# A recurrent attention layer and a two-layer MLP on one core: one step's value products set beside the next step's scores, and PSUM banks dealt out anew

## The chip, the cores and the metric

The program runs on one core of a Trainium2 chip. A core has TensorE (PE: matmuls, with its weight loads PEld), VectorE (DVE), ScalarE (ACT), GpSimdE (POOL) and SyncE (SP, which issues most DMAs). Matmuls write to PSUM, which has eight banks; the other engines work in SBUF and, except POOL, read PSUM. Engines run side by side, each executes its own instructions in order, and semaphores let one wait for another. The metric is the device time of the whole program in microseconds (us); lower is better.

## The reference

For each of 4 x 8 (batch, head) pairs a matrix memory is carried over 768 positions, 40 numbers wide, and read by the query. The output goes through two matrix products with a softplus between them.

```python
for t in range(S):                                  # q, k, v, o_gate: (4, 8, 768, 40)
    m_new  = np.maximum(f_gate[:, :, t] + m, i_gate[:, :, t])
    f_stab = np.exp(f_gate[:, :, t] + m - m_new);  i_stab = np.exp(i_gate[:, :, t] - m_new)
    C = f_stab * C + i_stab * einsum('bhd,bhe->bhde', vt, kt)
    n = f_stab * n + i_stab * kt
    denom = np.maximum(np.abs(n . qt), 1.0)
    y[:, :, t] = sigmoid(o_gate[:, :, t]) * (C . qt) / denom
x = y.transpose(0, 2, 1, 3).reshape(3072, 320)      # tokens x (head, dim)
out = softplus(x @ w_in) @ w_out                    # 320 -> 2048 -> 320, float32
```

## The kernel before, in words

**Tiles and steps.** The 3072 tokens are cut into 24 steps of 128 tokens (one batch entry b, one chunk c, all 8 heads; a step is written b_c). Three steps make a tile of the MLP: 8 tiles, 0 to 7. The order of the steps is 1_0, 2_0, 0_0 (tile 0), 3_0, 0_1, 0_2 (tile 1), 0_3 and so on; from step number 4 on, the chunks of one batch entry follow each other, so each step needs the state that the one before it leaves.

**The MLP.** A tile passes through 16 units f. A unit of the first layer is 8 matmuls of 384 columns into one PSUM tile `hp` (L978). ACT takes the softplus twice (`gh`, L854, and in place, L855), DVE takes the rounding rest `gl` = hp - gh (L858). The second layer multiplies gh and gl into three PSUM tiles `po` (L949, 9 matmuls of 320 columns); it runs two units behind, so PE alternates hp of unit f and po of unit f - 2. In tile 0 there is no gl: one softplus, and po in plain float32 in pairs of units. In this text hp4_3 is unit 3 of tile 4, gl4_3 its rest. An hp bank is free again when gl has been written (in tile 0, when gh has).

**The attention of a step** after tile 0. DVE scans the decays (`pw`, L439) and weighs the gates (`gw`, L491), POOL scales the values (`v`, L482; `vw`, L500), DVE scales the queries (`mv`, L381). PE then multiplies the **score group** (`sp`, two banks: state products L600, scores L606, 32 matmuls). DVE weighs the scores into mv (L611, four instructions), and two carries of the state follow, each a product on POOL (L564) and a sum on DVE (L567); the second sum waits for POOL, and POOL for the first sum. Then PE multiplies the **value group** (`yq`, one bank, L642, 16 matmuls), ACT copies it (L659), it goes through DRAM and comes back transposed (L664 to L679), and DVE and ACT make the tile's X of it (L683 to L698).

**PSUM.** Three pools: ps_h with the tag hp, ps_o with po0 to po2, ps_a for the attention. Each gives its buffers out in turn; an allocation waits for the readers of the tile that had the buffer before. At the start ps_h also holds wm, six `fb` tiles and three transposes `xp` (L706, one for each step of tile 0), in this order, before hp0_0. In the record, float32 matmuls show as two entries each.

**What sets the order.** The program is written out once, each engine's order then being fixed (`in_order`, L113). `products` (L922) counts PE's slots n; every other piece of work is a generator with due times, and `tick(n)` lets those run that are due. A step has a base (Q["B.."] up to step 11, later Q["S0".."S2"] + NB of its tile) and a table of offsets (W from tile 3 on; M, N before) with an entry for each part: SP for the score group, YQ for the value group, YD, RD, NM, FIN for what becomes of it, FB for the fetch of the decays. `later_step` (L806) turns the offsets into events. The first tile follows a table of its own, F.

Of the kernel before, what the change touches and what calls it, by code (L numbers as in the profile page):

```python
# [16 lines left out]
PSUM = bass.MemoryType.PSUM  # L17

B, H, S, D = 4, 8, 768, 40
# [5 lines left out]
NS = sum(SIZES)  # L25
START = [sum(SIZES[:t]) for t in range(NT + 1)]
# [9 lines left out]
EP = 48  # L36
MID = 0
WIDE = 3
FIRST = [(1, 0), (2, 0), (0, 0), (3, 0)]
ORDER = FIRST + [(b, c) for b in range(B) for c in range(NC) if (b, c) not in FIRST]  # L40
UW = 640
# [3 lines left out]
def mlstm_moe_kernel(  # L45
# [20 lines left out]
    stage = ctx.enter_context(tc.tile_pool(name="stage", bufs=2))  # L66

    dpool = ctx.enter_context(tc.tile_pool(name="dpool", bufs=1, space=bass.MemoryType.DRAM))
    ps_h = ctx.enter_context(tc.tile_pool(name="ps_h", bufs=3, space=PSUM))
    ps_o = ctx.enter_context(tc.tile_pool(name="ps_o", bufs=1, space=PSUM))  # L70
    ps_a = ctx.enter_context(tc.tile_pool(name="ps_a", bufs=2, space=PSUM))

    nc.scalar.preload_act_table_set("natural_log_exp_and_others")

# [37 lines left out]
    @contextmanager  # L112
    def in_order():  # L113

        traced = nc.cur_bb.bb.instructions
        first = traced[-1]
        yield
        start = next(k for k in reversed(range(len(traced))) if traced[k] is first) + 1
        last = {}
        for ins in traced[start:]:  # L120
            if ins.engine in last:
                tc.add_manual_dep(
                    ins,
                    last[ins.engine].name,
                    mybir.DependencyInfo(mybir.DependencyClass.NoSync, mybir.DependencyReason.DATA),
                    reason="in_order",
                )
            last[ins.engine] = ins
# [156 lines left out]
    def lows():  # L285

        yield Q["LB"]
        for u in range(NF // 2):
            wol[u] = wl.tile([128, 2, DM], F32R, tag="wo", name=f"wol{u}")
            nc.vector.tensor_tensor(wol[u], wof[u], woh[:, 2 * u : 2 * u + 2, :], op=ALU.subtract)  # L290
            yield -1000 - Q["LS"]

    W = dict(FB=-80, LOAD=-67, Y=-29, SCAN=4, VI=11, VW=16, IQ=20, SP=24, SPD=12, CN=31, CD=36, CE=37, CF=42, YQ=53,
             YQD=-32, EV=15, YD=61, YD1=3, RD=96, RY=11, RZ=1, NM=138, FIN=146, XH=19, XL=18)
    M = dict(FB=-23, LOAD=-50, Y=-9, SCAN=3, VI=-10, VW=10, IQ=25, SP=27, SPD=12, CN=33, CD=43, CE=49, CF=50, YQ=54,
             YQD=3, EV=47, YD=69, YD1=-30, RD=79, RY=-95, RZ=26, NM=116, FIN=128, XH=-9, XL=15)
    N = dict(FB=-26, LOAD=-57, Y=-7, SCAN=9, VI=-16, VW=22, IQ=23, SP=28, SPD=8, CN=30, CD=34, CE=39, CF=60, YQ=55,
             YQD=6, EV=17, YD=67, YD1=-32, RD=84, RY=-22, RZ=10, NM=125, FIN=150, XH=-9, XL=14)
    Q = dict(Gi0=68, Go0=50, Gi1=-42, Go1=1, Gi2=-47, Go2=36, Gi3=38, Go3=7, Gi4=6, Go4=18, Gi5=-8, Go5=31, Gi6=-10,
             Go6=7, Gi7=4, Go7=35, B3=40, B4=84, B5=125, B6=260, B7=300, B8=368, B9=446, B10=528, S0=-375, S1=-292,  # L300
             S2=-195, GT=-381, GL=52, LB=214, LS=33, SPD=-12, OF0=1, OF1=19, GR0=25, GR1=82, GR2=29, GR3=-26, GR4=18,
             GR5=38, LG=10, FS0=-51, FS1=25, FSW=-14, CI=-48, CO=-4, CS=34, K0=-23, K1=-29, CF=15, RC=-17, RS=92,
             B2=-20, B11=620, GT2=92, GL2=108, FS2=-31, GR6=-1, Hi0=-20, Ji0=63, Hi1=34, Ji1=78, Hi2=16, Ji2=34,
             Hi3=-12, Ji3=49, Hi4=-8, Ji4=-16, Hi5=36, Ji5=136, Hi6=-16, Ji6=107, Hi7=-67, Ji7=20)
    CI = dict(A=-6, B=2, C=-54, D=-2, E=10, F=30)
    CO = dict(A=3, B=-52, C=15, D=12, E=-36)
# [17 lines left out]
    class Step:  # L324
        def __init__(self, s):
# [4 lines left out]
            self.n = f"{self.b}_{self.c}"  # L330
            self.at = (M, M, N, W)[min(self.t, WIDE)]
            self.late = self.t > 1
# [51 lines left out]
    def wide_gates(ts):  # L384

        yield 0
        for t in ts:
            load_gates(t)
        yield Q["GL"]
        nc.scalar.preload_act_table_set("sigmoid_and_others")  # L390
        for t in ts:
            nc.scalar.activation(eg[t], eg[t], AF.Sigmoid)
            done.add(("eg", t))
        nc.scalar.preload_act_table_set("softplus")
# [3 lines left out]
    def load_gates(t):  # L398
        g, n = SIZES[t], 128 * 3 * L
        eg[t] = p1.tile([128, NG, 3, L], F32, tag="eg", bufs=2, name=f"eg{t}")[:, 0:g]  # L400
        src = oT[START[t] * n : START[t + 1] * n]
        nc.sync.dma_start(eg[t], src.rearrange("(p g c l) -> p g c l", g=g, c=3, l=L))
# [312 lines left out]
    def first_tile(follow):  # L715
# [17 lines left out]
        def next_gates():  # L733
            for t in range(1, WIDE):
                load_gates(t)
                yield
            for t in range(1, WIDE):
                nc.scalar.activation(eg[t], eg[t], AF.Sigmoid)
                done.add(("eg", t))
            yield  # L740
# [65 lines left out]
    def later_step(z):  # L806
        yw, at = values_wide(z), z.at
        c0, c1 = carry(z, 0), carry(z, 1)

        def fetch():  # L810
            decays(z)
            load_values(z)
            unpark(z)

        def y():
            for r in yw:
                if r == "write":
                    return
                yield r

        ev = [
            (at["FB"], fetch),
            (at["LOAD"], lambda: load(z)),
            (at["Y"], lambda: load_inter(z)),
            (at["SCAN"], lambda: decay(z)),
            (at["VI"], lambda: gate_values(z)),
            (at["VW"], lambda: last_decays(z)),
            (at["VW"], lambda: state_values(z)),
            (at["SP"], lambda: scores(z)),
            (at["YQ"], y),  # L830
            (at["YD"], lambda: yw),
            (at["RD"], lambda: read_wide(z)),
            (at["NM"], lambda: finish_wide(z)),
            (at["FIN"], lambda: end_wide(z)),
        ]
        ev += [
            (at["IQ"], lambda: scale_queries(z)),
            (at["CN"], lambda: next(c0)),
            (at["CD"], lambda: next(c0, None)),
        ]  # L840
        if z.c < NC - 1:
            ev += [(at["CE"], lambda: next(c1)), (at["CF"], lambda: next(c1, None))]
        yield from in_turn(ev)
# [17 lines left out]
    def convert(u, i):  # L861
        g = (weights_out if i else weights)(u)
        for k, w in (CO if i else CI).items():
            yield w
            next(g, None)
            if k == "C":
                yield -1000 - Q["CF"]
                fetch_next()
# [5 lines left out]
    def first_states():  # L874
        for w, k in zip((Q["FS0"], Q["FS1"], Q["FS2"]), (1, 0, 2)):
            yield w
            z = zs[k]
            state(z)
            yield -1000 - Q["FSW"]
            for _ in new_state(z):  # L880
                pass

    NB = [NF * (8 * t + 3 * START[t]) for t in range(NT)]
# [3 lines left out]
    def start(g, base):  # L887
        nonlocal order
        order += 1
        resume(g, base, 0, order)  # L890

    def resume(g, base, at, k):
        try:
            r = next(g)
        except StopIteration:
            return
        at = at - r - 1000 if r <= -1000 else max(at, base + r)
        heapq.heappush(queue, (at, k, base, g))
# [111 lines left out]
    def finished(t):  # L1010
        return all(s in ended for s in range(START[t], START[t + 1]))

    def whole(z):
        yield from later_step(z)
        ended.add(z.s)

    with in_order():
        for k, (u, i) in enumerate(tensors[AHEAD:]):
            start(convert(u, i), Q[f"K{k}"] if k < 2 else Q["CO" if i else "CI"] + Q["CS"] * u)
        start(first_states(), 0)  # L1020
        start(lows(), 0)
        rest = [Step(s) for s in range(START[1], NS)]
        for s in range(START[1], NS):
            z = rest[s - START[1]]
            base = Q[f"B{s}"] if s < START[4] else Q[f"S{z.g}"] + NB[z.t]
            start(whole(z), base)
        for t in range(WIDE, NT):
            start(wide_gates([t]), NB[t] + Q["GT"])
        zs = first_tile(rest[:3])
        products()  # L1030
# [52 lines left out]
```

## Time and profile before

| | us |
|---|---|
| median of three runs | 461.8 (461.75 to 463.18) |
| profiled execution | 461.91 |
| its span in the profile | 460.2 |
| PE busy | 433.4 (94%) |
| PEld busy | 402.9 (88%) |
| DVE busy | 303.9 (66%) |
| ACT busy | 211.2 (46%) |
| POOL busy | 137.2 (30%) |

The span is cut into 40 slices of 11.5 us in the page's second part; PE's digits there are 5756799 and then 9 to the end. So PE has gaps in the first 80 us, where weights are converted and tile 0 is prepared, and hardly any after. The chain of work that ended last is 81% PE by the page's fourth part, 36% hp (L978) and 34% po (L949), and 9% DVE. Outside the span lie 1.7 us of the profiled execution. The granted clock of TensorE is given as a share: 1.00 is 2.4 GHz, 0.50 is 1.2 GHz.

### The profile page before, as it was taken

The numbers are of one execution on the slowest core, as the hardware profiler recorded it, in microseconds if no ns is written. First come the engines' busy times: TensorE is split into PE (matmuls) and PEld (weight loads), VectorE is DVE, ScalarE is ACT, GpSimd is POOL, SyncE is SP. The second block draws the span as 40 slices with busy tenths as digits, with TensorE's granted clock in tenths as the row PEclk, the third lists the DMA queues.
The fourth block names the chain that finished last, engine by engine and source line by source line (L and its number), as shares of the span: only waits on it lengthen the run. The fifth ranks groups of instructions, "written<-read, shape, count | busy, mean of one in ns | idle before, by whom it ended". The sixth has DMA issues, their size and how long they took to land.

```text
span 460.2 us, 10555 instructions
## 1 busy us (share of the span) xinstructions
PE 433.4 (94%) x4266; PEld 402.9 (88%) x4266; DVE 303.9 (66%) x577; ACT 211.2 (46%) x416; POOL 137.2 (30%) x152
## 2 busy tenths in 40 slices
PE   5756799899999999999999999999999999999997
PEld 4555587677999999999999999999999999999996
DVE  4657488998987967766776867656876678242121
ACT  2727778784233642355333733463333543333332
POOL 8646078455531131233122312302223111000000
PEclk9975999999999999999999999999999999999999
DMA  7954967587656564654464263555374220101001
GB/s 200 333 188 115 274 197 246 147 214 168 178 180 182 154 151 122 164 144 96 150 185 117 74 204 108 129 143 138 105 196 129 78 78 19 41 0 46 0 1 43
DMA packets 38139, 62.55 MB, mean 136 GB/s; under 512 B 5626, under 2 KB 20258, under 8 KB 38090
## 3 DMA queue, kind: packets, MB, share of 16 engines
q1 hardware_dynamic: 25958, 53.62, 41.3%
q10 hardware_dynamic: 12132, 8.26, 6.3%
q8 instruction: 33, 0.54, 0.5%
q14 instruction: 16, 0.13, 0.1%
HBM read 53.60 MB, written 8.26 MB: 134 GB/s over the span
## 4 chain that ended last, share of the span: by engine, by line
PE 81%; DVE 9%; ACT 3%; POOL 3%; issue 2%; DMA 0%; SPq 0%; POOLq 0%; DVEq 0%; ACTq 0%
PE hp L978 36%; PE po L949 34%; PE yq L642 4%; PE sp L606 2%; PE sp L600 2%; POOL v L564 1%; DVE wof L236 1%; PE yp L619 1%; PE wm L723 1%; DVE wih L271 1%; PE fb L455 1%; DVE wil L269 1%; DVE mv L611 1%; DVE nm L685 1%; DVE gw L494 1%
## 5 line engine op out<-in xcount | busy, mean ns | idle before, releaser
L978 PE MATMUL hp<-X,wih 128*128 128x384 f32 x768 | 181.7, 344 | 4.0 <-ACT X L708 2.8
L978 PEld LDWEIGHTS hp<-X,wih 128*128 128x128 f32 x768 | 133.9, 189 | 9.0 <-ACT X L708 3.2
L854 ACT ACTIVATE gh<-hp 128x384 fp32r<-128x384 f32 x112 | 55.0, 491 | 181.8 <-PE hp L978 175.0
L858 DVE TENSOR_TENSOR gl<-hp,gh 128x384 fp32r<-128x384 f32 x112 | 61.6, 555 | 74.0 <-ACT hp L855 73.1
L949 PE MATMUL po<-wol,gh 128*128 128x320 f32 x336 | 71.2, 311 | 0.0
L949 PE MATMUL po<-woh,gl 128*128 128x320 f32 x336 | 70.3, 309 | 0.0
L949 PE MATMUL po<-woh,gh 128*128 128x320 f32 x336 | 69.8, 308 | 0.0
L978 PE MATMUL hp<-X,wil 128*128 128x384 f32 x256 | 66.6, 339 | 0.1
L500 POOL TENSOR_TENSOR vw<-vt,gw 128x328 f32<-128x328 f32 x23 | 21.7, 944 | 134.3 <-DVE gw L491 123.0
L564 POOL TENSOR_TENSOR v<-v,flast 40x328 f32<-40x328 f32 x37 | 38.2, 1032 | 69.4 <-DVE v L567 53.7
L949 PEld LDWEIGHTS po<-woh,gh 128*128 128x128 f32 x336 | 57.3, 188 | 0.1
L949 PEld LDWEIGHTS po<-woh,gl 128*128 128x128 f32 x336 | 54.9, 188 | 0.2
L949 PEld LDWEIGHTS po<-wol,gh 128*128 128x128 f32 x336 | 54.5, 188 | 0.5
L855 ACT ACTIVATE hp<-hp 128x384 f32<-128x384 f32 x112 | 54.5, 487 | 0.0
L978 PEld LDWEIGHTS hp<-X,wil 128*128 128x128 f32 x256 | 46.4, 189 | 0.9 <-DVE wil L269 0.5
L611 DVE TENSOR_TENSOR mv<-sp,pw 64x256 f32<-64x256 f32 x84 | 31.8, 417 | 14.7 <-PE sp L606 14.2
L482 POOL TENSOR_TENSOR v<-vt,gT 64x328 f32<-64x328 f32 x42 | 33.6, 801 | 22.5 <-DMA vt<-in_vko 19.6
L381 DVE TENSOR_TENSOR mv<-mv,fc 64x512 f32<-64x512 f32 (+1 forms) x42 | 39.1, 930 | 1.1 <-DMA fc<-fc_d 0.5
L949 PE MATMUL po<-wof,gh 128*128 128x320 f32 x96 | 28.5, 440 | 3.9 <-ACT v L544 2.7
L567 DVE TENSOR_TENSOR v<-v,sp 40x164 f32<-40x164 f32 x74 | 23.9, 323 | 12.0 <-POOL v L564 10.7
L439 DVE TENSOR_TENSOR_SCAN pw<-fb,near 128x512 f32<-128x512 f32 x21 | 26.4, 1255 | 3.8 <-DMA fb<-fz_d 3.8
L949 PEld LDWEIGHTS po<-wof,gh 128*128 128x128 f32 x96 | 17.6, 189 | 10.8 <-ACT v L544 3.0
(126 smaller groups left out, 439.9 us busy)
## 6 DMA issues: line engine op xcount, KB each, us to landing
qk<-in_qk SPq DMA_DIRECT2D x21, 416.0 KB
vt<-in_vko SPq DMA_DIRECT2D x23, 324.0 KB
fb<-fz_d SPq DMA_DIRECT2D x42, 128.0 KB
wi<-in_wts SPq DMA_DIRECT2D x8, 640.0 KB
wo<-in_wts SPq DMA_DIRECT2D x8, 640.0 KB
eg<-in_oT SPq DMA_DIRECT2D x7, 576.0 KB
out<-ob SPq DMA_DIRECT2D x24, 160.0 KB
yd<-y ACTq DMA_DIRECT2D x36, 96.0 KB
```

What stands on the lines that cost most here:

```text
L381: nc.vector.tensor_tensor(z.mv[ch][r], z.mv[ch][r], z.fc[r], op=ALU.mult)
L439: nc.vector.tensor_tensor_scan(pw.rearrange(flat), fb.rearrange(flat), eye.rearrange(flat), 0.0, ALU.mult, ALU.add)
L482: nc.gpsimd.tensor_tensor(vi, v1[r], g[r], op=ALU.mult)
L500: nc.gpsimd.tensor_tensor(z.vw, v1, z.gw.broadcast_to([128, H, E]), op=ALU.mult)
L564: nc.gpsimd.tensor_tensor(heads(whole), old, f, op=ALU.mult)
L567: nc.vector.tensor_tensor(dst[i], dst[i], z.cps[ch][dims(i)], op=ALU.add)
L611: nc.vector.tensor_tensor(half(z.mv[ch][r], i), sps[i][r], half(z.pw[r], i), op=ALU.mult)
L854: nc.scalar.activation(gh, hp, AF.Softplus)
L855: nc.scalar.activation(hp, hp, AF.Softplus)
L858: nc.vector.tensor_tensor(gl, hp, gh, op=ALU.subtract)
L949: nc.tensor.matmul(po[j], a[:, j * 128 : (j + 1) * 128], w, start=first, stop=(last and left[j] == 0))
L978: nc.tensor.matmul(hp, a, r, start=(i == 0), stop=(i == len(seq) - 1))
```

## The change

Three things. First, ps_h gets two banks instead of three, ps_a three instead of two. Second, from step JOIN = 9 (the first of tile 3, 1_1) to step 22, the offsets YQ, YD, RD, NM and FIN of a step are moved by one common shift, so that its YQ falls on the SP of the next step: the two groups are then issued back to back. Third, bases and FB are set anew: B9, B10, B11 by -28, -32, -46 slots, S0, S1, S2 by -60, -52, -59, FB of the table W from -80 to -60.

```diff
+JOIN = 9
...
-    ps_h = ctx.enter_context(tc.tile_pool(name="ps_h", bufs=3, space=PSUM))
+    ps_h = ctx.enter_context(tc.tile_pool(name="ps_h", bufs=2, space=PSUM))
     ps_o = ctx.enter_context(tc.tile_pool(name="ps_o", bufs=1, space=PSUM))
-    ps_a = ctx.enter_context(tc.tile_pool(name="ps_a", bufs=2, space=PSUM))
+    ps_a = ctx.enter_context(tc.tile_pool(name="ps_a", bufs=3, space=PSUM))
...
-    W = dict(FB=-80, LOAD=-67, Y=-29, SCAN=4, VI=11, VW=16, IQ=20, SP=24, SPD=12, CN=31, CD=36, CE=37, CF=42, YQ=53,
+    W = dict(FB=-60, LOAD=-67, Y=-29, SCAN=4, VI=11, VW=16, IQ=20, SP=24, SPD=12, CN=31, CD=36, CE=37, CF=42, YQ=53,
...
+    def place(s):
+        z = rest[s - START[1]]
+        return Q[f"B{s}"] if s < START[4] else Q[f"S{z.g}"] + NB[z.t]
...
+    rest = [Step(s) for s in range(START[1], NS)]
...
         for s in range(START[1], NS):
             z = rest[s - START[1]]
-            base = Q[f"B{s}"] if s < START[4] else Q[f"S{z.g}"] + NB[z.t]
-            start(whole(z), base)
+            if s >= JOIN and s + 1 < NS:
+                shift = place(s + 1) + rest[s + 1 - START[1]].at["SP"] - place(s) - z.at["YQ"]
+                z.at = {**z.at, **{k: z.at[k] + shift for k in ("YQ", "YD", "RD", "NM", "FIN")}}
+            start(whole(z), place(s))
```

Line numbers after the change are one higher than before (L978 becomes L979). POOL's order is the same in both programs, and PE's order is the same up to hp1_10.

**Place 1, PE at the start of tile 0.** Before, with the semaphore that each row waits for; x0_0 is the third step's x, hp0_2 and hp0_3 are units of the first layer:

```order
L706 MATMUL xp2_0_355<-ident4_79,x2_0_352 128x128
L706 MATMUL xp2_0_355<-ident4_79,x2_0_352 128x128 [waits DVE_49]
L706 MATMUL xp0_0_369<-ident4_79,x0_0_349 128x128 [waits Activation_49]
L706 MATMUL xp0_0_369<-ident4_79,x0_0_349 128x128 x2
L978 MATMUL hp0_0_407<-X0_303,wih_104 128x384 [waits DVE_49,Activation_49]
```

```order
L978 MATMUL hp0_2_478<-X0_303,wih_104 128x384 [waits PE_49]
L978 MATMUL hp0_2_478<-X0_303,wih_104 128x384 x4
L978 MATMUL hp0_2_478<-X0_303,wil_105 128x384 x2
L978 MATMUL hp0_2_478<-X0_303,wih_104 128x384
L978 MATMUL hp0_3_495<-X0_303,wih_104 128x384 [waits Activation_49]
L539 MATMUL cp1_0_497<-vw1_0_395,k1_0_125 40x41 [waits Pool_49]
```

The same rows after:

```order
L707 MATMUL xp2_0_355<-ident4_79,x2_0_352 128x128
L707 MATMUL xp2_0_355<-ident4_79,x2_0_352 128x128 [waits DVE_49]
L707 MATMUL xp0_0_369<-ident4_79,x0_0_349 128x128 [waits DVE_49]
L707 MATMUL xp0_0_369<-ident4_79,x0_0_349 128x128 x2
L979 MATMUL hp0_0_407<-X0_303,wih_104 128x384 [waits DVE_49,Activation_49]
```

```order
L979 MATMUL hp0_2_478<-X0_303,wih_104 128x384 [waits Activation_49]
L979 MATMUL hp0_2_478<-X0_303,wih_104 128x384 x4
L979 MATMUL hp0_2_478<-X0_303,wil_105 128x384 x2
L979 MATMUL hp0_2_478<-X0_303,wih_104 128x384
L979 MATMUL hp0_3_495<-X0_303,wih_104 128x384 [waits Activation_49]
L540 MATMUL cp1_0_497<-vw1_0_395,k1_0_125 40x41 [waits Pool_49]
```

The order is the same; what a row waits for is not. The transposes xp0_0 now wait for DVE instead of ACT (the buffer's last user is the transpose xp1_0, read last by DVE in L710, instead of an fb tile), and hp0_2 waits for ACT (gh of hp0_0) instead of PE. The wait of hp0_3 is on ACT in both, but its buffer is now that of hp0_1, and before it was that of hp0_0.

**Place 2, PE in tile 4.** Before, where the value group of step 2_3 begins; its neighbours are matmuls of the second layer (the score group of 2_3 stood alone inside hp4_1):

```order
L949 MATMUL po4_0_3420<-woh_106,gl4_0_3384 128x320
L949 MATMUL po4_1_3421<-woh_106,gl4_0_3384 128x320
L949 MATMUL po4_2_3422<-woh_106,gl4_0_3384 128x320
L642 MATMUL yq2_3_3437<-mv0_2_3_3239,v0_0_110 64x64
L642 MATMUL yq2_3_3437<-mv0_2_3_3239,v0_0_110 48x64
L642 MATMUL yq2_3_3437<-mv1_2_3_3240,v1_0_111 64x64
```

After, the end of the same value group:

```order
L643 MATMUL yq2_3_3469<-mv0_2_3_3135,v0_0_110 64x64
L643 MATMUL yq2_3_3469<-mv0_2_3_3135,v0_0_110 48x64
L643 MATMUL yq2_3_3469<-mv1_2_3_3136,v1_0_111 64x64
L643 MATMUL yq2_3_3469<-mv1_2_3_3136,v1_0_111 48x64
L601 MATMUL sp0_2_4_3488<-vw2_4_3452,vt2_4_3305 40x41
L601 MATMUL sp1_2_4_3489<-vw2_4_3452,vt2_4_3305 40x41 x2
L601 MATMUL sp0_2_4_3488<-vw2_4_3452,vt2_4_3305 40x41 x2
```

The value group now ends where the score group of step 2_4 begins. There are 14 such pairs; up to step 8 the groups stand apart as before.

**Place 3, DVE in tile 1.** Before, from the rest of unit 10 on; sp of step 1_1 stands behind gl of unit 11:

```order
L858 TENSOR_TENSOR gl1_10_1712<-hp1_10_1652,gh1_10_1669 128x384
L491 TENSOR_TENSOR gw1_1_1735<-gT_100,pw1_1_1706 128x8
L698 TENSOR_TENSOR X2_1603<-eg2_367,X2_1603 128x3x128
L381 TENSOR_TENSOR mv1_1_1_1619<-mv1_1_1_1619,fc1_1_1620 64x512
L381 TENSOR_TENSOR mv0_1_1_1618<-mv0_1_1_1618,fc1_1_1620 40x512
L858 TENSOR_TENSOR gl1_11_1751<-hp1_11_1687,gh1_11_1708 128x384
L611 TENSOR_TENSOR mv0_1_1_1618<-sp0_1_1_1755,pw1_1_1706 64x256
L611 TENSOR_TENSOR mv0_1_1_1618<-sp1_1_1_1756,pw1_1_1706 64x256
```

After:

```order
L859 TENSOR_TENSOR gl1_10_1756<-hp1_10_1654,gh1_10_1675 128x384
L612 TENSOR_TENSOR mv0_1_1_1535<-sp0_1_1_1706,pw1_1_1632 64x256
L612 TENSOR_TENSOR mv0_1_1_1535<-sp1_1_1_1707,pw1_1_1632 64x256
L612 TENSOR_TENSOR mv1_1_1_1536<-sp0_1_1_1706,pw1_1_1632 64x256
L612 TENSOR_TENSOR mv1_1_1_1536<-sp1_1_1_1707,pw1_1_1632 64x256
L568 TENSOR_TENSOR v1_1_113<-v1_1_113,sp0_1_1_1706 40x164 x2
L568 TENSOR_TENSOR v0_0_110<-v0_0_110,sp1_1_1_1707 40x164 x2
L699 TENSOR_TENSOR X2_1610<-eg2_367,X2_1610 128x3x128
L859 TENSOR_TENSOR gl1_11_1802<-hp1_11_1704,gh1_11_1752 128x384
```

The weighing of step 1_1 and both its carries now stand between gl1_10 and gl1_11, with the last pass over X2 (L699) behind them. In the same way the weighing and both carries stand directly in front of gl3_3, gl4_3 and gl5_3 (and of gl3_14, gl4_14, gl5_14, whose unit holds the pair). In front of gl2_8, gl3_8 and gl5_8 only the first carry stands.

## Rows read from the trace of the kernel before

**Rows 1.** Windows: stretch, length; busy us of PE, PEld, DVE, ACT, POOL; granted clock; DMA share, GB/s.

```profile
21.80:25.10 3.30, 3.30 (x17) 3.30 (x17) 0.00 (x1) 0.00 (x0) 0.00 (x0) 0.50 1.00 232
32.10:45.60 13.50, 6.97 (x38) 5.36 (x38) 9.84 (x17) 8.59 (x13) 10.15 (x11) 0.50 0.47 139
260.00:320.00 60.00, 60.00 (x660) 57.72 (x660) 41.08 (x81) 25.26 (x53) 14.38 (x16) 1.00 0.48 133
```

**Rows 2.** Waits of PE: us in total, times, longest us.

```profile
PE sp L585 <- DVE pw L574: 2.6, 1, 2.6
PE po L949 <- DVE wof L236: 1.2, 2, 1.0
...
PE sp L600 <- POOL vw L500: 0.5, 1, 0.5
```

**Rows 3.** Timeline of PE in tile 3: start, us, operation, count.

```profile
242.31 1.03 PE L978 MATMUL hp<-X,wih 128*128 128x384 f32 x5
...
245.01 1.03 PE L978 MATMUL hp<-X,wih 128*128 128x384 f32 x5
...
248.59 0.51 PE L978 MATMUL hp<-X,wil 128*128 128x384 f32 x2
249.03 0.52 PE L600 MATMUL sp<-vw,vt 64*40 64x41 f32 x32
...
249.97 0.45 PE L978 MATMUL hp<-X,wih 128*128 128x384 f32 x1
250.26 0.60 PE L949 MATMUL po<-woh,gh 128*128 128x320 f32 x3
...
254.32 0.51 PE L978 MATMUL hp<-X,wih 128*128 128x384 f32 x2
254.76 1.15 PE L642 MATMUL yq<-mv,v 104*64 104x64 f32 x32
255.83 0.79 PE L978 MATMUL hp<-X,wih 128*128 128x384 f32 x3
256.46 0.51 PE L978 MATMUL hp<-X,wil 128*128 128x384 f32 x2
```

**Rows 4.** Timeline of PE at the start; in brackets idle before and releaser.

```profile
35.83 1.70 PE L706 MATMUL xp<-ident,x 128*128 128x128 f32 x6 [5.96 <-DVE x L629]
40.34 0.69 PE L978 MATMUL hp<-X,wih 128*128 128x384 f32 x1 [2.80 <-ACT X L708]
...
48.57 0.44 PE L978 MATMUL hp<-X,wih 128*128 128x384 f32 x1 [0.27 <-ACT gh L850]
...
50.85 0.34 PE L978 MATMUL hp<-X,wih 128*128 128x384 f32 x1
53.85 3.50 PE L949 MATMUL po<-wof,gh 128*128 128x320 f32 x12 [2.66 <-ACT v L544]
```

**Rows 5.** Timeline of ACT at the start.

```profile
48.03 0.49 ACT L850 ACTIVATE gh<-hp 128x384 f32<-128x384 f32 x1
...
52.10 0.48 ACT L850 ACTIVATE gh<-hp 128x384 f32<-128x384 f32 x1
...
53.21 0.59 ACT L544 COPY v<-cp 40x164 f32<-40x164 f32 x2
```

**Rows 6.** Timeline of DVE at the start.

```profile
39.31 0.56 DVE L710 TENSOR_TENSOR X<-xp,X 128x384 fp32r<-128x384 f32 x1
...
61.66 1.53 DVE L611 TENSOR_TENSOR mv<-sp,pw 64x256 f32<-64x256 f32 x4 [1.32 <-PE sp L606]
```

**Rows 7.** Timeline of DVE behind the score group of 249.03.

```profile
250.10 1.53 DVE L611 TENSOR_TENSOR mv<-sp,pw 64x256 f32<-64x256 f32 x4 [2.04 <-PE sp L606]
251.66 0.66 DVE L567 TENSOR_TENSOR v<-v,sp 40x164 f32<-40x164 f32 x2
253.27 0.66 DVE L567 TENSOR_TENSOR v<-v,sp 40x164 f32<-40x164 f32 x2 [0.95 <-POOL v L564]
253.96 0.56 DVE L858 TENSOR_TENSOR gl<-hp,gh 128x384 fp32r<-128x384 f32 x1
```

More of the change, by code (lines that the diff above doesn't have):

```diff
@@ L299, in mlstm_moe_kernel @@
     Q = dict(Gi0=68, Go0=50, Gi1=-42, Go1=1, Gi2=-47, Go2=36, Gi3=38, Go3=7, Gi4=6, Go4=18, Gi5=-8, Go5=31, Gi6=-10,
-             Go6=7, Gi7=4, Go7=35, B3=40, B4=84, B5=125, B6=260, B7=300, B8=368, B9=446, B10=528, S0=-375, S1=-292,
-             S2=-195, GT=-381, GL=52, LB=214, LS=33, SPD=-12, OF0=1, OF1=19, GR0=25, GR1=82, GR2=29, GR3=-26, GR4=18,
+             Go6=7, Gi7=4, Go7=35, B3=40, B4=84, B5=125, B6=260, B7=300, B8=368, B9=418, B10=496, S0=-435, S1=-344,
+             S2=-254, GT=-381, GL=52, LB=214, LS=33, SPD=-12, OF0=1, OF1=19, GR0=25, GR1=82, GR2=29, GR3=-26, GR4=18,
              GR5=38, LG=10, FS0=-51, FS1=25, FSW=-14, CI=-48, CO=-4, CS=34, K0=-23, K1=-29, CF=15, RC=-17, RS=92,
-             B2=-20, B11=620, GT2=92, GL2=108, FS2=-31, GR6=-1, Hi0=-20, Ji0=63, Hi1=34, Ji1=78, Hi2=16, Ji2=34,
+             B2=-20, B11=574, GT2=92, GL2=108, FS2=-31, GR6=-1, Hi0=-20, Ji0=63, Hi1=34, Ji1=78, Hi2=16, Ji2=34,
              Hi3=-12, Ji3=49, Hi4=-8, Ji4=-16, Hi5=36, Ji5=136, Hi6=-16, Ji6=107, Hi7=-67, Ji7=20)
@@ L1021, in mlstm_moe_kernel @@
         start(lows(), 0)
-        rest = [Step(s) for s in range(START[1], NS)]
         for s in range(START[1], NS):
             z = rest[s - START[1]]
-            base = Q[f"B{s}"] if s < START[4] else Q[f"S{z.g}"] + NB[z.t]
-            start(whole(z), base)
+            if s >= JOIN and s + 1 < NS:
+                shift = place(s + 1) + rest[s + 1 - START[1]].at["SP"] - place(s) - z.at["YQ"]
+                z.at = {**z.at, **{k: z.at[k] + shift for k in ("YQ", "YD", "RD", "NM", "FIN")}}
+            start(whole(z), place(s))
         for t in range(WIDE, NT):
```

## The prediction

> **What bounds the kernel now.** I read the windows first. In 260 to 320 us PE is busy 60.00 of 60.00 us at clock 1.00, with DVE at 41.1 and ACT at 25.3 [rows 1]. So from some point on a change is worth what it takes from PE's own sequence, less every wait that it brings to PE. The waits of PE come next: from 60 us on the list holds little, 1.2 us for DVE's weights (L236), 0.5 for POOL's vw, and two of 0.8 and 0.5 us more [rows 2]. Last come PE's timelines. One unit of hp and po takes 245.01 - 242.31 = 2.70 us [rows 3]; shared out over 8 x 384 and 9 x 320 columns that is 0.174 us for an hp matmul, 0.145 for a po matmul. At the start PE is not the bound: it idles 5.96 us before the transposes xp, 2.80 before hp0_0 and 2.66 before the first po [rows 4].
>
> **What a pair saves.** The value group of 254.76 follows two hp matmuls that began at 254.32, so it starts 254.76 - 254.32 - 0.35 = 0.09 late. Its record lasts 1.15 and a last entry some 0.22, so the last starts at 255.69 and hp follows at 255.83, 0.14 later where the group's own rhythm is 0.03 (1.15 - 0.22 over 31). The three hp matmuls after it take 0.63 instead of 0.52 [rows 3]. Going in and out of a small group thus costs 0.09 + 0.11 + 0.11 = 0.31 us. The score group shows the same: from 248.59 to 250.26 are 1.67 us, of which three hp matmuls are 0.52. A pair goes in and out once instead of twice, but has an edge between its groups that the trace does not show. Its nearest row is the way in, from hp's 128 x 128 shape to the group's 104 x 64: 0.09. I take that; a free edge and one as dear as a way out (0.22) are the ends. A pair saves 0.22 (0.09 to 0.31), and 14 pairs **-3.1** (-1.3 to -4.3).
>
> The value rows are 104 x 64 and 128 x 64, the score rows 64 x 40 and 40 x 64 [rows 3]. The Trainium skill (TensorEngine Tiling (Array Packing), Key Properties) says that a change of the tiling mode, not just of the tile, drains TensorE. By that rule the edge is a third change of mode, as dear as a way out, and the pairs would give -1.3; by the row of the way in they give -3.1. No run here shows this edge; the sum would be 467 by the rule.
>
> **What two banks cost at the start.** The xp of the third step now waits until DVE has read that of the first, 39.31 + 0.56 = 39.87 [rows 6]. Before, it ran straight behind the second, six matmuls in 1.70 [rows 4]. Three of them take about 0.9 to 1.1, ACT's cast about 0.48 (by a gh of the same shape [rows 5]), so hp0_0 starts near 41.4 instead of 40.34: +1.1. ACT's work behind that cast has no gap until 49, so gh of hp0_0 ends at 48.03 + 0.49 + 1.1 = 49.6 and gh of hp0_1 at 52.10 + 0.48 + 1.1 = 53.7 [rows 5]. hp0_3 waited for the first of these before (48.57 [rows 4]), and now it waits for the second. From its first to its last matmul were 50.85 - 48.57 = 2.28, since the state products stand in between, so po can start at 53.7 + 0.05 + 2.28 + 0.17 = 56.2 instead of 53.85 [rows 4]. The copies of those products on ACT, which held po before (53.21 + 0.59 [rows 5]), end just ahead of that. That is **+2.3** (+1.2 if the transposes cost nothing). Does it last? DVE waits at 61.66 for a score group of PE behind that po [rows 6] and from then on works nearly without a break to 110 us, so it shifts along and PE's later waits do not soak it up.
>
> **What they cost in tile 1.** hp1_12 needs the bank that gl1_10 frees, hp1_13 that of gl1_11. Between these DVE now does the weighing, both carries with POOL's round trip, and a pass over X2. Rows 7 give the price: from the start of the weighing to the end of the following gl 253.96 + 0.56 - 250.10 = 4.42, plus 0.56 for X2 (by the pass over X of the same size [rows 6]): 5.0. PE needs 2.70 for the unit between. So it waits some 2.3 (0.5 if DVE is ahead of PE there, 3.0 if POOL is slow). The wait of 0.5 for vw [rows 2] belongs to this same step, whose place changes: I count it as gone. **+1.8**.
>
> **What they cost later.** Count from the start of hp4_3: hp 1.39, one po 0.15, way in 0.09, so the value group starts at 1.63, lasts 0.96, edge 0.09, scores from 2.68. The weighing starts 250.10 - 249.03 = 1.07 behind the scores' start [rows 3, 7], at 3.75, and gl4_3 ends 4.42 later at 8.17. PE is through the scores at 2.68 + 0.94 = 3.62, then eight po (1.16 + 0.11) and hp4_4 and nine po (2.70) to 7.59, and hp4_5 needs that bank. It waits 8.17 + 0.05 - 7.59 = 0.6. Three units have this form (gl3_3, gl4_3, gl5_3): **+1.9**. Where gl stands in front of the second carry (gl2_8, gl3_8, gl5_8) the same count gives 7.4 against 7.5, and where the pair stands inside the unit (gl3_14, gl4_14, gl5_14) 7.3 to 7.6 against 7.6; DVE's queue in front of these decides, for six places **+0.5** (0 to +2). The third bank of ps_a ends no wait: no wait of PE in the list is for a reader of attention's banks [rows 2]. The DMAs that the new bases move go a few us to either side of old ones, behind loads that land well ahead; no PE wait hangs on them, so 0.
>
> **Sum.** -3.1 + 2.3 + 1.8 + 1.9 + 0.5 = +3.4. The profiled execution took 461.91, 0.1 above the median of 461.8: 465.3, **465.2** against the median. What a measurement here can tell from no change is 0.3%, 1.4 us (460.4 to 463.2).
>
> **Rivals.**
> - *The clock falls at the start.* PE would idle some 2.4 us ahead of hp0_2 and 2.6 ahead of hp0_3, with one unit of 1.4 between. The trace has 0.50 at 21.8 to 25.1 after a wait of 2.6, and at 32.1 to 45.6 around one of 5.96 [rows 1, 2, 4]; against it, the clock stayed up through the 2.66 ahead of po. At 0.50, hp0_3 to hp0_5 and the first po would run at half speed, 5.4 us for 2.7: 467.9. Chance 0.22.
> - *It cancels.* The places on DVE are met without waits, as by the count six of nine nearly are, and tile 1 costs 0.5: -3.1 + 2.3 + 0.5 - 0.5 + 0.5 = -0.3, some 461.6. For it speaks that DVE has 19 of 60 us free [rows 1]; against it, that the work of a step comes in one lump of 4.42. Chance 0.18.
> - *Faster.* The edge is free (-4.3) and the start's delay goes into the waits of PE for weights between 75 and 100 us (2.5 us, 1.2 of them for L236 [rows 2]), because ACT and POOL, which prepare these weights, do not wait for PE. DVE's place at 61.66 decides: if its idle 1.32 there is not lengthened, this holds. Then -4.3 + 2.3 - 2.0 + 1.0 for banks: 458.8. Against it: DVE's weights stand in order behind that wait. Chance 0.14.
> - The forecast itself, 463.5 to 466.8: chance 0.46.
>
> **How the numbers follow.** Faster by over 0.3%: the third rival, 0.14. Within 0.3%: most of the second, 0.15. Slower: the forecast, the first rival and the rest, 0.71. The range of 460.8 to 469.0 holds the forecast, the clock's case with a dear edge or a longer low stretch, and most of the second rival.
>
> **What the profile after would show.** hp0_0 near 41.4, and waits of PE for ACT gh (L851) of 2.4 and 2.6 us at 47 to 54; the first po near 56. A wait of hp (L979) for DVE gl (L859) of about 2 us in tile 1 and of 0.6 in tiles 3, 4 and 5. Fourteen pairs of about 2.2 us from the hp or po before to the one behind, in place of 1.15 + 1.28. If hp waits nowhere for gl, the tile 1 and later terms were wrong; if the po starts near 54, the start was; if the pairs take 2.4, the edge was; a second stretch at 0.50 around 52 would be the clock's case.

## The result, and the profile after

The changed kernel took 468.39 us (median of 5 runs, 466.51 to 473.96) against 461.8 before (460.62 to 463.18): a ratio of 1.013 (95% interval 1.0108 to 1.0152). It is slower, as forecast; the forecast of 465.2 had the direction and half of the size, and 468.39 lies near the upper end of the range. Run again beside the experiments, the kernel took 469.05 against 462.06, 1.0145 (1.0113 to 1.0176). One execution here (473.96), one of not_joined and one of start_bank were disturbed: the ratios and the medians of the experiments' table leave these out, and the rows here are of an undisturbed execution of 466.72 us, run beside the experiments. Line numbers are one higher than before.

A reader who compares times in two traces needs a common anchor. The first transposes xp began at 35.83 before [rows 4] and begin at 33.53 here. Up to there both programs give the same instructions in the same order, and carries_later below, which starts like the changed kernel, begins them at 36.28. So I take these 2.3 us as luck of this execution. Its span of 465.0 is 4.8 above before, and with the start set level 7.1, which agrees with the medians (7.0).

The waits of PE (us in total, times, longest), to be held against [rows 2]:

```profile
PE xp L707 <- DVE x L630: 6.3, 2, 6.0
...
PE hp L979 <- DVE gl L859: 3.8, 7, 1.9
PE hp L979 <- ACT gh L851: 1.9, 2, 1.1
PE hp L979 <- ACT X L709: 1.4, 1, 1.4
...
PE xp L707 <- DVE X L711: 1.2, 1, 1.2
PE hp L979 <- DVE X L699: 0.9, 1, 0.9
```

The waits for gl did not exist before. The one of the xp and the two for gh are the two banks at the start (one wait for gh, of 0.27, existed before); the wait of hp0_0 for X has shrunk from 2.8 to 1.4.

PE at the start (start, us, operation, count; idle before and releaser), which answers to [rows 4]:

```profile
33.53 1.06 PE L707 MATMUL xp<-ident,x 128*128 128x128 f32 x3 [5.97 <-DVE x L630]
35.75 0.90 PE L707 MATMUL xp<-ident,x 128*128 128x128 f32 x3 [1.16 <-DVE X L711]
38.04 0.69 PE L979 MATMUL hp<-X,wih 128*128 128x384 f32 x1 [1.39 <-ACT X L709]
...
46.28 1.97 PE L979 MATMUL hp<-X,wih 128*128 128x384 f32 x5 [0.78 <-ACT gh L851]
...
50.34 0.69 PE L979 MATMUL hp<-X,wih 128*128 128x384 f32 x1 [1.14 <-ACT gh L851]
...
54.40 3.39 PE L950 MATMUL po<-wof,gh 128*128 128x320 f32 x12
```

On the time scale of before, the first po lies at 54.40 + 2.30 = 56.70. The transposes of the third step wait for DVE, as forecast, but 1.16 and not the some 3 us that the forecast's 39.87 means. They follow DVE's pass over the first xp, which ends at 35.70 here; its twin before is the pass of 37.44, and the forecast took the next one, of 39.31 [rows 6]:

```profile
35.14 0.56 DVE L711 TENSOR_TENSOR X<-xp,X 128x384 fp32r<-128x384 f32 x1 [0.35 <-ACT X L709]
```

```profile
37.44 0.56 DVE L710 TENSOR_TENSOR X<-xp,X 128x384 fp32r<-128x384 f32 x1 [0.35 <-ACT X L708]
```

So hp0_0 starts 38.04 - 33.53 = 4.51 behind the first transposes, and before it was 40.34 - 35.83 = 4.51. ACT shows that the 1.16 is covered:

```profile
36.86 0.76 ACT L226 ACTIVATE sgo<-wo 128x640 uint32<-128x640 uint8 x1
37.53 0.46 ACT L709 CAST X<-xp 128x384 fp32r<-128x384 f32 x1
...
49.81 0.48 ACT L851 ACTIVATE gh<-hp 128x384 f32<-128x384 f32 x1
```

The cast that hp0_0 waits for stands behind other work of ACT, which ends 4.09 behind the first xp in both traces (37.62 - 33.53 here, 39.92 - 35.83 before), with or without the delay.

The clock (windows: stretch, length; busy us of PE, PEld, DVE, ACT, POOL; granted clock; DMA share, GB/s), which answers to [rows 1]:

```profile
31.50:54.00 22.50, 16.01 (x90) 12.68 (x91) 13.32 (x22) 15.40 (x29) 9.25 (x10) 0.50 0.69 193
54.50:60.00 5.50, 5.50 (x27) 4.55 (x26) 3.32 (x3) 3.50 (x6) 4.13 (x5) 1.00 0.46 145
260.00:320.00 60.00, 59.35 (x657) 57.10 (x655) 39.77 (x83) 27.28 (x54) 13.50 (x17) 1.00 0.52 140
```

Before, the stretch at 0.50 ended near 45.7; now it goes on to 54. In the steady part PE is idle for 0.65 of 60 us, where it was never idle.

A pair in tile 3, which answers to [rows 3]:

```profile
241.88 0.31 PE L950 MATMUL po<-woh,gl 128*128 128x320 f32 x1
242.12 1.15 PE L643 MATMUL yq<-mv,v 104*64 104x64 f32 x32
243.19 0.52 PE L601 MATMUL sp<-vw,vt 64*40 64x41 f32 x32
243.53 0.67 PE L607 MATMUL sp<-qk 40*64 40x64 f32 x32
244.13 0.57 PE L950 MATMUL po<-woh,gl 128*128 128x320 f32 x2
```

From the value group to the scores are 1.07, the 1.07 that lay before between a value group and the hp behind it (255.83 - 254.76 [rows 3]); the scores take their old 0.94. So the edge is a last step of 0.15 in a group whose own step is 0.03: it costs 0.12, between the way in (0.09) and the way out (0.22). What a pair saves is one way in and one slow stretch behind: 0.20.

DVE in tile 1, from the rest of unit 10 to that of unit 11:

```profile
148.09 0.55 DVE L859 TENSOR_TENSOR gl<-hp,gh 128x384 fp32r<-128x384 f32 x1
148.56 1.52 DVE L612 TENSOR_TENSOR mv<-sp,pw 64x256 f32<-64x256 f32 x4
150.11 0.66 DVE L568 TENSOR_TENSOR v<-v,sp 40x164 f32<-40x164 f32 x2
151.71 0.66 DVE L568 TENSOR_TENSOR v<-v,sp 40x164 f32<-40x164 f32 x2 [0.94 <-POOL v L565]
152.41 0.56 DVE L699 TENSOR_TENSOR X<-eg,X 128x384 fp32r<-128x384 f32 x1
153.00 1.11 DVE L859 TENSOR_TENSOR gl<-hp,gh 128x384 fp32r<-128x384 f32 x2
```

and the two matmuls of PE that such a lump holds up, hp1_13 and hp3_5:

```profile
153.61 1.14 PE L979 MATMUL hp<-X,wih 128*128 128x384 f32 x5 [1.94 <-DVE gl L859]
...
231.38 1.14 PE L979 MATMUL hp<-X,wih 128*128 128x384 f32 x5 [0.44 <-DVE gl L859]
```

The wait ends when gl1_11 is written, at 153.56, the 5.0 behind the start of the weighing that [rows 7] gave. The five matmuls behind a wait take 1.14 instead of 1.03 [rows 3], so each wait costs at least 0.11 more than its idle time.

### The profile page after: what moved, and what is told of

Read it like the earlier page. It is cut to its first block, busy times and chain, and to the rows that moved or that the text cites. A ratio compares the mean times of both kernels' runs of the same rounds, so it can differ in the third digit from the quotient of the medians.

```text
span 472.2 us, 10537 instructions
## 1 busy us (share of the span) xinstructions
PE 439.5 (93%) x4266; PEld 408.6 (87%) x4266; DVE 300.4 (64%) x577; ACT 210.8 (45%) x416; POOL 131.0 (28%) x152
## 4 chain that ended last, share of the span: by engine, by line
PE 55%; DVE 22%; DMA 10%; issue 4%; POOL 3%; ACT 3%; SPq 1%; ACTq 1%; DVEq 0%; POOLq 0%
PE hp L979 26%; PE po L950 23%; DMA nw<-yd 6%; DVE mv L612 3%; DVE mv L382 2%; PE yq L643 2%; DVE nm L686 2%; DVE gl L859 2%; DVE v L568 2%; DMA yd<-y 2%; POOL v L565 1%; DVE eg L695 1%; PE sp L607 1%; DMA og<-in_vko 1%; DVE pw L440 1%
## 5 line engine op out<-in xcount | busy, mean ns | idle before, releaser
L979 PE MATMUL hp<-X,wih 128*128 128x384 f32 x768 | 185.1, 348 | 10.7 <-DVE gl L859 5.9
L979 PEld LDWEIGHTS hp<-X,wih 128*128 128x128 f32 x768 | 136.2, 192 | 18.2 <-DVE gl L859 8.4
L950 PE MATMUL po<-woh,gl 128*128 128x320 f32 x336 | 71.4, 312 | 0.0
L950 PE MATMUL po<-woh,gh 128*128 128x320 f32 x336 | 71.3, 311 | 0.0
L950 PE MATMUL po<-wol,gh 128*128 128x320 f32 x336 | 70.2, 310 | 0.0
L979 PE MATMUL hp<-X,wil 128*128 128x384 f32 x256 | 67.4, 343 | 0.3 <-DVE wil L270 0.3
L565 POOL TENSOR_TENSOR v<-v,flast 40x328 f32<-40x328 f32 x37 | 33.6, 907 | 79.8 <-DVE v L568 70.9
L501 POOL TENSOR_TENSOR vw<-vt,gw 128x328 f32<-128x328 f32 x23 | 20.7, 902 | 123.8 <-DVE nm L684 66.9
L979 PEld LDWEIGHTS hp<-X,wil 128*128 128x128 f32 x256 | 47.6, 193 | 0.8 <-DVE wil L270 0.7
L382 DVE TENSOR_TENSOR mv<-mv,fc 64x512 f32<-64x512 f32 (+1 forms) x42 | 34.7, 826 | 2.6 <-DMA fc<-fc_d 2.0
L643 PEld LDWEIGHTS yq<-mv,v 128*48 128x48 f32 (+3 forms) x672 | 21.4, 130 | 5.2 <-issue 4.9
```

The source lines that it names most:

```text
L382: nc.vector.tensor_tensor(z.mv[ch][r], z.mv[ch][r], z.fc[r], op=ALU.mult)
L565: nc.gpsimd.tensor_tensor(heads(whole), old, f, op=ALU.mult)
L643: nc.tensor.matmul(yq[i * PP : i * PP + m, p, rows(ch)], z.v[ch][k, h * E : h * E + m], z.mv[ch][k, h, :], start=True, stop=True,)
L950: nc.tensor.matmul(po[j], a[:, j * 128 : (j + 1) * 128], w, start=first, stop=(last and left[j] == 0))
L979: nc.tensor.matmul(hp, a, r, start=(i == 0), stop=(i == len(seq) - 1))
```

## The experiments

Theory A is the forecast's: what PE waits for in front of hp, with two banks, outweighs the pairs. B: the new bases cost the time. C: the clock at the start. All ratios are to the kernel before, run beside.

| kernel | us | ratio (95% interval) |
|---|---|---|
| again: the change | 469.05 | 1.0145 (1.0113 to 1.0176) |
| banks_only | 471.61 | 1.0211 (1.0165 to 1.0258) |
| join_old_banks | 486.46 | 1.0542 (1.0491 to 1.0594) |
| bases_only | 463.37 | 1.0029 (1.0007 to 1.0050) |
| not_joined | 473.91 | 1.0222 (1.0177 to 1.0267) |
| start_bank | 465.91 | 1.0080 (1.0057 to 1.0103) |
| carries_later | 465.88 | 1.0073 (1.0048 to 1.0099) |
| both | 463.34 | 1.0022 (1.0002 to 1.0042) |
| sums_last | 461.73 | 0.9986 (0.9968 to 1.0005) |
| even_bases | 463.15 | 1.0025 (1.0003 to 1.0047) |
| clear_gl | 459.16 | 0.9940 (0.9920 to 0.9959) |

**again.** The changed kernel without an edit.

> The changed kernel once more, for a profile to compare with. Theory A (the banks of ps_h bring waits that outweigh the pairs): 468, with waits of hp for gl of about 2 us in tile 1 and 0.6 to 1.0 in each of tiles 2 to 5, some 6 in all, and 3 us at the start. Theory B (the new bases, not the banks, cost the time: DMAs and X come late): 468 as well, but with waits of PE for attention's inputs, and gaps of ACT behind DMAs in tile 1. Theory C (the clock at the start): most of the 6 us lie ahead of 60 us from the start, in a stretch at 0.50 that ends near 57 instead of 45.7.

A is borne out in kind: 3.8 us of waits for gl in seven places, where some 6 were expected, and 2.7 at the start. C is partly seen: the low stretch ends at 54, but most of the loss lies behind 60 us. Of B's late inputs PE shows one, 0.9 for X (L699).

**banks_only.**

```diff
-    ps_h = ... name="ps_h", bufs=3
+    ps_h = ... name="ps_h", bufs=2
-    ps_a = ... name="ps_a", bufs=2
+    ps_a = ... name="ps_a", bufs=3
```

> The kernel before with two banks in ps_h and three in ps_a, nothing joined and no base moved. A: 468 to 471: 3.2 at the start as in the changed kernel, and what in the trace of before starts less than a gl ahead of the second next hp: about 1.5 in tile 1, 1.9 in tile 2, 1.3 in each of tiles 4 to 6. B: 465, the start's 3 alone. C: the whole loss ahead of 60 us, 465 to 467.

The banks alone cost 2.1%, a little above A's 468 to 471; the waits in tiles 2 and 4 to 6 are there, the 1.5 in tile 1 is not. The waits of PE:

```profile
PE hp L978 <- DVE gl L858: 5.5, 8, 1.7
...
PE hp L978 <- ACT gh L850: 4.9, 2, 2.5
```

Here the clock came back at 41 us and fell a second time, behind waits of 2.48 and 2.40 for gh:

```profile
42.00:51.00 9.00, 4.11 (x46) 3.25 (x47) 3.29 (x7) 6.25 (x13) 0.00 (x0) 1.00 0.92 274
51.50:54.50 3.00, 3.00 (x9) 2.70 (x9) 1.40 (x2) 1.95 (x6) 0.75 (x2) 0.50 1.08 248
```

That is the order of events of the prediction's first rival, but not its price: hp0_4 begins 23.83 behind the first xp, as in the changed kernel (23.85), and before it was 21.12. In the changed kernel's trace the clock had not come back before, so the hp matmuls ran longer, and the waits for gh were 0.78 and 1.14.

**join_old_banks.** The change with its banks as before (ps_h 3, ps_a 2).

> The changed kernel with ps_h back at three banks and ps_a at two. The pairs and the bases stay. Each score group then waits inside the pair until ACT has copied the value group in front of it (0.59 and two semaphores, some 0.7). A: -3.1 for the pairs, 14 x 0.7 = +9.8 for that wait, no wait of hp: 468; without that wait it would be 458.7. B: above 470, since the cost of the bases comes on top.

A miss: 486, not 468. The wait inside the pair is there (13.8 in 12 places), but once a tile it is 1.74 to 2.28 instead of some 0.5. In four of these five cases ACT has the next gates ahead of the copy, with two loads of tables of 1.28 each. Then this follows (PE in tile 5):

```profile
320.42 1.15 PE L643 MATMUL yq<-mv,v 104*64 104x64 f32 x32
321.49 0.27 PE L601 MATMUL sp<-vw,vt 64*40 64x41 f32 x2
323.87 0.71 PE L601 MATMUL sp<-vw,vt 64*40 64x41 f32 x27 [2.11 <-ACT y L660]
...
326.92 1.00 PE L950 MATMUL po<-woh,gh 128*128 128x320 f32 x3
...
331.29 0.60 PE L950 MATMUL po<-woh,gh 128*128 128x320 f32 x3
```

```profile
324.00:330.00 6.00, 6.00 (x78) 5.88 (x79) 3.06 (x9) 1.38 (x3) 1.57 (x3) 0.50 0.92 211
332.00:338.00 6.00, 6.00 (x40) 6.00 (x39) 1.35 (x3) 2.33 (x6) 0.00 (x0) 1.00 0.14 38
```

Three po matmuls take 1.00 at 0.50 and 0.60 after. The trace has five such stretches, of 3.4 to 6.8 us, one behind each of the five long waits and none behind the seven of 0.5. The third bank of ps_a is thus what lets the two groups follow each other without a wait, and with ps_o taking three of the eight it can only come from ps_h.

**bases_only.** The change with ps_h 3, ps_a 2 and JOIN past the last step.

> The kernel before with the new bases B9 to B11, S0 to S2 and FB alone: three banks for hp, two for attention, nothing joined. A: 461 to 463, as before: the bases cost nothing. B: 464 to 466.

+1.3 (0.3 to 2.3), between A and B. PE waits 2.9 us in four places for vw (L501), 0.5 before. The longest, 1.44 at 177.68, is read back on DVE:

```profile
173.74 0.56 DVE L695 TENSOR_TENSOR eg<-yx,eg 128x384 f32<-128x384 f32 x1 [3.18 <-DMA yx<-yd]
...
176.27 0.16 DVE L492 TENSOR_TENSOR gw<-gT,pw 128x8 f32<-128x8 f32 x1
```

DVE stands 3.18 us at a pass that waits for the value group's way through DRAM; gw, which vw needs, is queued behind it. Before, DVE stood once so, 2.59 at 145.19. This profile is of the slowest of the ten runs (465.65), so it shows where the time goes and not how much.

**not_joined.** The change with JOIN past the last step: its banks and its bases alone.

> The changed kernel with its banks and its bases, but no value group moved (JOIN past the last step). A: the pairs are worth 14 x 0.20 = 2.8, so 471.8 (470.5 to 473), with the gl waits as they are or a little larger, since a value group on its own stands in the way of a weighing's unit. Rival (the joining brings the waits, since the scores now come behind the value group): 466 to 468.

473.9, so the pairs are worth 4.9 of medians, or 3.6 (1.0 to 6.1) by the ratios of runs beside each other; 2.8 was expected, and the rival falls. The waits for gl differ as well, 5.7 in its profile (3.6 of it at hp4_0, hp5_0 and hp6_0) and 3.8 in the change's, so this difference is not the pairs' alone.

**start_bank.** hp0_2 alone takes a bank of ps_a.

```diff
+                pool, tag = (ps_a, "pa") if (t, f) == (0, 2) else (ps_h, "hp")
-                hp = ps_h.tile([128, T], F32, tag="hp", ...
+                hp = pool.tile([128, T], F32, tag=tag, ...
```

> The changed kernel (469.05 in the run beside the first experiments) with one allocation moved: hp0_2 takes a bank of ps_a, so that hp0_2 waits for nothing and hp0_3 again for gh of hp0_0. Theory A (the two banks cost 2.7 at the start, and this stays until the end): -2.7, 466.3, with no wait for gh (L851) of over 0.3. Rival (the start is soaked up later, or the clock stays low there whatever the banks): 468 to 469.

-3.1, close to A; one wait for gh of 0.43 is left, and the clock is at 1.00 from 45.5 on. The start's loss lasts to the end unless it is mended there.

**carries_later.** The sums of both carries move behind the gl that they stood in front of.

```diff
-    W = dict(..., CN=31, CD=36, CE=37, CF=42, YQ=53,
+    W = dict(..., CN=31, CD=44, CE=45, CF=52, YQ=53,
```

> The changed kernel with the offsets CD, CE, CF of table W at 44, 45, 52 instead of 36, 37, 42: DVE's sums of the two carries fall behind the gl that they stood in front of, in tile 1 and after. Theory A: the waits of hp for gl (3.8 in seven places, with a slow matmul behind each some 4.5) nearly go: 464.5. Rival: DVE is full there, another wait takes their place (vw, the state, X), 467 to 469.

-3.2 instead of -4.5. The waits at hp3_5, hp4_5 and hp5_5 are gone and that at hp1_13 nearly is, but hp1_15, which needs gl1_13, now waits 1.7.

**both.** The two edits together.

> Both edits together. A: the terms add, 469.05 - 2.7 - 4.5 = 461.9, level with before; what then stays above 459 (the kernel before less 2.8 for the pairs) is what the new bases cost, 1.3 by the run of the bases alone, and the start's rest. Rival (one hides the other): 464 or more.

463.3: the terms add within the noise (-3.1 and -3.2 make 462.7), and the rest above the kernel before is in tiles 1 and 2. DVE, ahead of gl1_13 and of gl2_8:

```profile
153.78 0.23 DVE L684 TENSOR_SCALAR nm<-nw 128x128 f32<-128x128 f32 x1 [1.76 <-DMA nw<-yd]
...
190.78 0.23 DVE L684 TENSOR_SCALAR nm<-nw 128x128 f32<-128x128 f32 x1 [2.28 <-DMA nw<-yd]
```

The same kind of wait as in bases_only, now with a gl queued behind it: hp1_15, hp2_10 and hp2_11 wait.

**sums_last and even_bases.** Both add to the two edits; the first moves NM of steps 8 and 10, the second that of step 8 and the bases.

```diff
+            z.at = {**z.at, "NM": z.at["NM"] + {8: 11, 10: 7}.get(s, 0)}
```

```diff
-  B9=418, B10=496, ... B11=574
+  B9=440, B10=512, ... B11=583
+            z.at = {**z.at, "NM": z.at["NM"] + {8: 11}.get(s, 0)}
```

> The kernel with both edits (463.34), and NM of two steps later (step 8 by 11 slots, step 10 by 7), so that DVE's instructions that wait for the value group's way through DRAM (nm, which waited 1.76 and 2.28 us for the DMA of nw there) stand behind gl1_13 and gl2_8 instead of in front. Theory A, extended (with two banks each thing that DVE waits for in front of a gl comes to PE): hp2_0's 1.25, and the 0.85 and 0.42 at hp2_10 and hp2_11 go: 461, and the spread of the runs gets smaller. Rival (the remainder is due to the bases, which crowd tile 1): 463.

> The kernel with both edits, NM of step 8 later by 11 slots, and the bases of steps 9 to 11 spread evenly between those of step 8 and step 12 (440, 512, 583 instead of 418, 496, 574). Theory A: the same waits go, 461, as in the kernel beside it. Theory B (the bases of the change crowd tile 1, where DVE has no break): lower than the kernel beside it by 0.5 to 1.5, 459.5 to 460.5, which is what the pairs are worth below the kernel before (462.05 - 2.8 = 459.3).

The first is level with before, and its twelve runs lie within 3.4 us (5.7 in both). The wait of hp1_15 (which the expectation calls hp2_0's) is gone and that of hp2_10 too, but hp2_11 now waits 1.7, since nm and the first pass over X stand in front of gl2_9. The second is no better (463.15), against theory B; its waits for gl are 2.7 at hp2_6, hp2_11 and hp4_10. Since it leaves NM of step 10 where it was, it does not test the bases by themselves.

**clear_gl.** Two offsets of step 10, so that they stand behind gl2_9 as well.

```diff
+            z.at = {k: v + {8: {"NM": 11}, 10: {"NM": 26, "FIN": 19}}.get(s, {}).get(k, 0) for k, v in z.at.items()}
```

> The kernel before last (461.73) with nm and the first pass over X of step 10 later still (NM by 26 slots in all, FIN by 19), so that they stand behind gl2_9, where hp2_11 waited 1.7 for them. Theory A: -1.9 with the slow matmul behind the wait: 459.8, below before (462.1) by what the pairs are worth (2.8) less a rest of waits; ratio 0.995. Rival (the time of tile 2 is bound by the work of DVE and its DMAs, and a late X comes back as a wait at hp3_0): 461.5 to 462.

459.16 against 462.16 beside it, 0.6% (0.4 to 0.8) faster than the kernel before, and its eight runs lie within 1.9 us (458.71 to 460.65), where the twelve of both spread over 5.7. What is left of PE's waits for X and for gl:

```profile
PE hp L980 <- DVE X L699: 0.4, 1, 0.4
...
PE hp L980 <- DVE gl L859: 0.2, 1, 0.2
```

From tile 3 on each tile, with three pairs, gains 0.66 to 0.73 on the kernel before. So the pairs are worth 0.22 to 0.24 each once nothing waits.

## Why the prediction was right in direction and half in size

- **Pairs, -3.1:** -2.8 by the edge in the trace, -3.2 by clear_gl's tiles. The edge came out at 0.12, a little above the 0.09 taken. The Trainium skill's rule (TensorEngine Tiling (Array Packing), Key Properties), that a change of mode drains TensorE, has the trace half on its side: the step costs what the first step of a way out does (0.12 and 0.11), but no slow matmuls follow it, and the pairs did not shrink to -1.3.
- **Start, +2.3:** the first po comes 54.40 - 33.53 = 20.87 behind the first xp, 18.02 before: +2.85. The size is nearly right by two errors that offset each other, which is luck. hp0_0 was not late at all (+1.1 forecast): the forecast read the wrong one of DVE's three passes (39.31 for 37.44), and a delay of 1.16 ends before ACT comes to the cast. By its own count +1.2 would then be left. And hp0_3 with the state products took 54.40 - 50.34 = 4.06 to the first po instead of some 2.45, at a clock of 0.50: 1.6 more. That it lasts to the end was right: it is +2.8 at hp1_0, and start_bank gives it back.
- **The clock's rival** was given 0.22, and half of it happened. The clock did not fall anew in the change's trace but stayed low until 54, some 20.5 behind the first xp, where it was 9.8 before; in banks_only it fell anew. Its price lay inside the start's term instead of on top of it. The Trainium skill (TensorE: Matmul & The Clock Gate, A second HAM failure mode: psum-queue depth-cycling) says that short idles between groups which cycle through PSUM banks can make the clock swing. Of the kernels here, join_old_banks has such a swing, five times, but each behind a single wait of 1.74 to 2.28; the change's trace has none in its steady part.
- **Tile 1, +1.8:** 1.94 of idle for 2.3 forecast, which moves the starts by 2.1, 0.3 more at hp1_15, 0.11 behind each, and vw's wait gone as forecast (0.4 by starts): +2.2. The 0.3 has another source than the carries, which the step below names.
- **The head of tile 1, not forecast:** hp1_0 waits 0.95 for X (L699), and the starts move by 1.1. Two instructions of DVE ahead of it took longer than before: the one of L237 1.36 instead of 0.82, the pass over X 1.09 instead of 0.55. The pass, here and before:

```profile
106.37 1.09 DVE L699 TENSOR_TENSOR X<-eg,X 128x384 fp32r<-128x384 f32 x1
```

```profile
105.28 0.55 DVE L698 TENSOR_TENSOR X<-eg,X 128x384 fp32r<-128x384 f32 x1
```

No wait for a DMA stands there, and not_joined, with the same banks and bases, has no such wait of PE (clear_gl has 0.41). So it is not put down to banks or bases; why the two take longer stays open.
- **Later, +2.4:** PE's order in the changed kernel is that of clear_gl, where PE waits nowhere in these tiles, so each matmul can be set beside its twin. hp3_5, hp4_5 and hp5_5 wait, as forecast: late by 0.6 each (0.44 of it shown as idle), as forecast, and by 0.11 more for the slow matmuls, which the forecast did not count: 2.1 for 1.9. Of the six other places hp2_10, hp4_10 and hp5_10 are late by 0.35, 0.38 and 0.23, and 0.11 behind each: 1.3 for 0.5, within the forecast's 0 to 2. Small delays of hp at the heads of tiles 4 to 6 and in tile 3, none over 0.2, add 0.7. Together +4.1.
- **The step that failed** in kind, and not only in size, is the last of the part on later costs: the bases, "no PE wait hangs on them, so 0". bases_only measures them at +1.3: DVE's passes that wait for the value group's way through DRAM come too early in DVE's queue, and what stands behind them (gw and vw, or a gl) is late. In the change's trace DVE waits so at nm 5.9 us in five places, before at none. Four of them stand in front of gl1_13, gl2_8, gl4_8 and gl5_8:

```profile
155.70 0.23 DVE L684 TENSOR_SCALAR nm<-nw 128x128 f32<-128x128 f32 x1 [1.59 <-DMA nw<-yd]
...
191.55 0.23 DVE L684 TENSOR_SCALAR nm<-nw 128x128 f32<-128x128 f32 x1 [1.10 <-DMA nw<-yd]
...
290.32 0.23 DVE L684 TENSOR_SCALAR nm<-nw 128x128 f32<-128x128 f32 x1 [0.85 <-DMA nw<-yd]
...
342.66 0.23 DVE L684 TENSOR_SCALAR nm<-nw 128x128 f32<-128x128 f32 x1 [1.61 <-DMA nw<-yd]
```

These are the rests that hp1_15, hp2_10, hp4_10 and hp5_10 wait for, 1.7 in all by starts, which the terms of tile 1 and later hold already. For the first two sums_last shows it: with nm moved, both waits are gone. In tiles 4 and 5 it is argued from the place in the queue, where nm is one part of the lump: carries_later and clear_gl move only the carries there, and clear_gl has no wait at hp4_10 and hp5_10. not_joined has one wait at nm (1.4), so there the moved offsets of the value group bring it rather than the bases.
- By terms, with the pairs as in clear_gl: -3.2 + 2.8 + 1.1 + 2.2 + 4.1 = 7.0, of 7.1 in this trace (6.6 to 7.0 by medians). So of the 3.6 that the forecast of 3.4 lacked here the later waits are the largest part (1.7), then the head of tile 1 (1.1), the start (0.5) and tile 1 (0.4); the pairs came out 0.1 better. The bases' 1.3 is no term beside these.
- What stays open: why the time ahead of the first xp differs by 2.3 between executions of the same instructions; why two instructions of DVE took longer at the head of tile 1; and what the bases cost in the change itself. Their 1.3 was measured with the old banks and without the pairs, and not_joined against banks_only, the same bases with the new banks, gives 0.5 with an interval of some 3 either way.

## What to carry to other kernels

A PSUM bank taken from the engine that sets the time is paid for where some other engine's queue holds a lump in front of the instruction that frees the bank; list what stands there, with what each item itself waits for, before moving the bank. The kernel came out 3 us below the one before only after those lumps (the sums of the carries, nm and a pass over X behind a DMA) had been moved behind that instruction and one bank had been given back at the start. A profile's idle time understates a wait (0.44 of idle at hp3_5 went with 0.7 of time): count by the starts of matmuls, with the slow ones behind the wait, and look at the granted clock there.

## What the runs showed of the hardware that was not expected

- Like waits of PE end differently: 2.11 inside a pair was followed by 0.50 for 6.8 us (join_old_banks), 1.94 between large matmuls by no fall of the clock (again); but in the changed kernel's execution of 473.96 a wait of 1.93 at the same hp1_13, which ended at 158.30, was followed by 0.55 over 3.5 us.
- The Trainium skill (Perfetto Trace Analysis, Optimization Strategy) says that a gap which repeats on the engine that should be saturated can mean too few buffers for the next tile. The repeated 0.44 at hp3_5, hp4_5 and hp5_5 is such a gap, and the kernel before, with three banks, has none there; carries_later ended it with two banks, by the order of DVE's queue alone.
